# The first MoE in five token blocks instead of six, its temporaries in hand-made rings

## Chip, cores and metric

One core of a Trainium2 chip runs the whole program. The metric is the device time of one execution in microseconds. Engines: PE is the matmul engine (TensorE), PEld its weight loads, DVE the vector engine, ACT the scalar engine, POOL GpSimd, and SP the queue that issues the DMAs.

## What is computed

Attention with a forget bias, then two mixture blocks without routing, on 4 x 576 = 2304 tokens of 512 features:

```python
x = attention(q, k, v, s)                       # 2304 x 512
gate = 1 / (1 + exp(-(x @ w_gate)))             # first MoE, 1536 hidden
x = (gate * (x @ w_val)) @ w_out                # 2304 x 512
h = x @ w_in                                    # second MoE, 2048 hidden
out = (h * cos(h)) @ w_out2                     # 2304 x 512
```

The weights of both MoEs come as 64-bit floats.

## The kernel before

The attention is ordered by a planner at build time (`Plan`, L118) and ends at about 185 us. What follows it, `moe()` (L799), is written out by hand: every engine takes its instructions in the order of two loops, and semaphores make it wait for its operands.

Each value x is kept as two 32-bit parts, a rounded one and the rest (XH and XL, gh and gl, the halves of a weight piece `wp`), and a product is three matmuls, high x high, high x low and low x high (`mm3`, L378). XH and XL hold all tokens, feature by feature: [128, 4, 2304].

The first MoE works on blocks of TB = 384 tokens, NB = 6 of them, and on hidden tiles of 128, 12 of them in six groups (`GROUPS1`, L360: 1, 2, 2, 2, 3 and 2 tiles). `work` (L389) makes the list of items: group by group, in it block by block, in it tile by tile; 72 items. An item's matmuls are `gate_val` (24: gate and value, each 4 feature chunks x 3) and `down1` (12: 4 output chunks x 3). The weights are the stationary side, so a matmul streams the tokens of a block: 384 columns.

The loop at L943 runs one item ahead: `gate_val(i)`, then `down1(i-1)`. Then follow the other engines' instructions: `glu` (ACT: sigmoid sg, L812; DVE: product g, L814; ACT: cast gh, L816), `evac1` of item i-1 (on the last tile of a group its four output chunks are added to `acc`: by ACT copies in the first group, L842, by DVE else, L844 and L846, in the last group with XH by ACT, L848, and XL by POOL, L849, put off to `drain_late`), `glu_lo` (DVE: difference gl, L822), and `background(share)`.

`background` decodes the weights of the next group. A piece (a 128 x 512 tile of a weight) is fetched by a DMA from SP (L308) into one of two `raw` buffers and then takes five operations, among them DVE's L312, L317, L321, L325 and L333, ACT's L313, and POOL's L326 and L334. The number of operations per item, `share`, is set at the first item of a group (L956 to L966): five times the pieces, divided by the items that are left, rounded up.

```python
share = -(-share // (NB * len(GROUPS1[it["gi"]]) - 1))
```

The temporaries come from pools: gh and gl four buffers each (`gp`), sg and g two each and kk one (`tp`), all of 384 columns. Matmul results live in the eight banks of PSUM (one tile, `pw`): four in turn for gate and value, four for the down sums.

The second MoE (L972) has 96 items of the same 384-token blocks: `up2` (12 matmuls of 384 columns), three items later `down2` (9 matmuls of 512 columns, here the tokens are stationary), between them `phase` (ACT: kk, L865), `cosine` (DVE: L870, L871; ACT: L872, L873), `gated` (DVE: L879) and `gated_split` (ACT: gh, L885; POOL: gl, L886). `acc` is used again, in pieces of 512 columns (`evac2`: L907, L909, L914).

Of the kernel before, what the change touches and what calls it, by code (L numbers as in the profile page):

```python
# [244 lines left out]
def kernel(  # L245
# [137 lines left out]
    def xmm(ps, w, b):  # L383
        cols = slice(b * TB, (b + 1) * TB)
        for c in range(NDC):
            fs = slice(c * P, (c + 1) * P)
            mm3(ps[:, 0:TB], w[:, 0, fs], w[:, 1, fs], XH[:, c, cols], XL[:, c, cols], c == 0, c == NDC - 1)

    def work(groups):  # L389
        items = []  # L390
        for gi, gr in enumerate(groups):
            for b in range(NB):
                for fc in gr:
                    items.append(dict(b=b, f=fc, gi=gi, first=fc == gr[0], last=fc == gr[-1], g0=gi == 0, g1=gi == len(groups) - 1))
        return items

    def gate(it):
        it["ps"] = [b[:, 0:TB] for b in pair_a()]
        xmm(it["ps"][0], W["g", it["f"]], it["b"])

    def val(it):
        xmm(it["ps"][1], W["v", it["f"]], it["b"])
# [5 lines left out]
    items1, items2 = work(GROUPS1), work(GROUPS2)  # L408
# [390 lines left out]
    def moe():  # L799
        with ExitStack() as c2:  # L800
            gp = c2.enter_context(tc.tile_pool(name="gp", bufs=4))
            tp = c2.enter_context(tc.tile_pool(name="tp", bufs=2))
# [3 lines left out]
            acc = accp.tile([P, NB, NDC * TB], F32, name="acc")  # L806


            def glu(it):
                pg, pv = it.pop("ps")  # L810
                sg = tp.tile([P, TB], F32, name="sg")
                act.activation(sg, pg, AF.Sigmoid)  # L812
                g = tp.tile([P, TB], F32, name="g")
                dve.tensor_tensor(g, pv, sg, ALU.mult)  # L814
                gh = gp.tile([P, TB], F32R, name="gh")
# [3 lines left out]
            def glu_lo(it):  # L819
                gh, g = it["g"]  # L820
                gl = gp.tile([P, TB], F32R, name="gl")
# [5 lines left out]
            def down1(it, c):  # L827
# [5 lines left out]
                mm3(px[b, c][:, 0:TB], w[:, 0, fs], w[:, 1, fs], gh, gl, it["first"], it["last"])  # L833

            def evac1(it, c):
                b = it["b"]
                if not it["last"]:
                    return
                ps = px.pop((b, c))[:, 0:TB]
                a = acc[:, b, c * TB:(c + 1) * TB]  # L840
# [4 lines left out]
                else:  # L845
                    dve.tensor_tensor(a, ps, a, ALU.add)  # L846
                    xh = XH[:, c, b * TB:(b + 1) * TB]
                    act.copy(xh, a)  # L848
                    late.append(lambda: pool.tensor_tensor(XL[:, c, b * TB:(b + 1) * TB], a, f(xh), ALU.subtract))  # L849
# [6 lines left out]
            def up2(it):  # L856
                b, fc = it["b"], it["f"]
                ph = banks(2, 0, 3)
                xmm(ph, W["i2", fc], b)
                it["ps"] = ph[:, 0:TB]  # L860

            def phase(it):
                h = it["ps"]
                it["kk"] = kk = tp.tile([P, TB], I32, name="kk", bufs=1)
                act.mul(kk, h, 1.0 / (2.0 * math.pi))  # L865

            def cosine(it):
                h, kk = it["ps"], it.pop("kk")
                r = tp.tile([P, TB], F32, name="sg")
# [172 lines left out]
```

## Time and profile before

| | us |
|---|---|
| median of 3 runs | 1045.12 (1044.97 to 1045.98) |
| span of the profiled execution, first to last instruction | 1043.9 |
| PE busy | 1030.7 (99%) |
| PE weight loads busy | 945.7 (91%) |
| DVE busy | 733.4 (70%) |
| ACT busy | 471.9 (45%) |
| POOL busy | 442.0 (42%) |

The profiled execution's own time is known by its span alone; the three timed runs lie 1.1 to 2.1 us over it. Busy times of different engines overlap. PE's matmuls overlap each other as well, so their price is read from the distance between two starts and not from the duration of one. Attention takes the first 185 us, the first MoE the time to about 640, the second the rest.

### The profile page before, as it was taken

Reading aid. Unit: us, or ns where it says so; the run is one execution under the profiler, and the core shown is the slowest. Engines: PE = TensorE matmul, PEld = TensorE weight load, DVE = VectorE, ACT = ScalarE, POOL = GpSimd, SP = SyncE. Lnnn points to the kernel's source line nnn. Section 1 sums busy time; section 2 is a strip of 40 time slices with the busy share of each in tenths; the row PEclk is TensorE's granted clock in tenths of the full one; section 3 lists DMA queues with packets and bytes.
Section 4 is the critical chain, followed back from the end, with each engine's and each line's share of the span. In section 5 each row is a group of like instructions: output and inputs, shape, how many; then the busy total and the mean of one; then the engine's idle time right before and its main releaser. Section 6 shows DMA issues by size and latency. Waiting matters only on the chain.

```text
span 1043.9 us, 16751 instructions
## 1 busy us (share of the span) xinstructions
PE 1030.7 (99%) x6116; PEld 945.7 (91%) x6116; DVE 733.4 (70%) x1382; ACT 471.9 (45%) x1060; POOL 442.0 (42%) x518
## 2 busy tenths in 40 slices
PE   8999999999999999999999999999999999999998
PEld 6776777899999999999999999899999999999997
DVE  7788898576646657744443886987688878886565
ACT  4877877342222222222221334666555455544443
POOL 3567876242302214411110674655355535552222
PEclk9999999999999999999999999999999999999999
DMA  7786783221101112201100111111011101100111
GB/s 173 171 194 163 192 183 98 90 84 41 62 21 61 41 41 78 66 22 39 41 21 21 61 62 41 41 61 42 21 61 41 54 28 41 60 2 8 53 61 61
DMA packets 94802, 70.49 MB, mean 68 GB/s; under 512 B 61888, under 2 KB 82752, under 8 KB 94720
## 3 DMA queue, kind: packets, MB, share of 16 engines
q1 hardware_dynamic: 93456, 69.06, 23.8%
q8 instruction: 48, 0.79, 0.3%
q10 hardware_dynamic: 1264, 0.37, 0.2%
q14 instruction: 34, 0.28, 0.1%
HBM read 64.54 MB, written 4.87 MB: 66 GB/s over the span
## 4 chain that ended last, share of the span: by engine, by line
PE 81%; DVE 9%; issue 3%; ACT 3%; POOL 2%; DMA 2%; SPq 0%; DVEq 0%; ACTq 0%; POOLq 0%
PE pw L380 17%; PE pw L381 17%; PE pw L379 17%; PE pw L896 6%; PE pw L898 6%; PE pw L897 6%; PE pw L726 3%; PE pw L687 3%; PE pw L628 3%; PE pw L633 1%; DVE wm L321 1%; POOL XL L849 1%; DVE wm L325 1%; DVE g L814 1%; DVE gl L822 1%
## 5 line engine op out<-in xcount | busy, mean ns | idle before, releaser
L380 PE MATMUL pw<-XL,wp 128*128 128x384 f32 x960 | 322.7, 336 | 0.0
L381 PE MATMUL pw<-XH,wp 128*128 128x384 f32 x960 | 322.7, 336 | 0.0
L379 PE MATMUL pw<-XH,wp 128*128 128x384 f32 x960 | 322.6, 336 | 0.0
L379 PEld LDWEIGHTS pw<-XH,wp 128*128 128x128 f32 x960 | 180.1, 188 | 3.8 <-DVE g L879 0.2
L380 PEld LDWEIGHTS pw<-XL,wp 128*128 128x128 f32 x960 | 180.0, 188 | 3.6
L326 POOL TENSOR_TENSOR wm<-wm,wx 128x512 int32<-128x512 int32 x68 | 90.6, 1332 | 212.6 <-DVE wm L325 211.3
L381 PEld LDWEIGHTS pw<-XH,wp 128*128 128x128 f32 x960 | 180.1, 188 | 0.0
L886 POOL TENSOR_TENSOR gl<-g,gh 128x384 fp32r<-128x384 f32 x96 | 108.7, 1133 | 150.9 <-ACT gh L885 150.7
L334 POOL TENSOR_TENSOR wp<-wm,wp 128x512 fp32r<-128x512 f32 x68 | 101.4, 1491 | 156.7 <-DVE wp L333 149.5
L814 DVE TENSOR_TENSOR g<-pw,sg 128x384 f32<-128x384 f32 x72 | 40.0, 556 | 145.1 <-PE pw L381 132.6
L898 PE MATMUL pw<-wp,gl 128*128 128x512 f32 x288 | 112.2, 390 | 0.5 <-POOL gl L886 0.5
L896 PE MATMUL pw<-wp,gh 128*128 128x512 f32 x288 | 112.2, 389 | 0.1
L897 PE MATMUL pw<-wp,gh 128*128 128x512 f32 x288 | 112.1, 389 | 0.0
L816 ACT CAST gh<-g 128x384 fp32r<-128x384 f32 x72 | 37.0, 514 | 146.7 <-DVE g L814 146.7
L871 DVE SCALAR_TENSOR_TENSOR sg<-kk,sg 128x384 f32<-128x384 int32 x96 | 100.5, 1047 | 3.3
L872 ACT ACTIVATE sg<-sg 128x384 f32<-128x384 f32 x96 | 50.5, 526 | 107.4 <-DVE sg L871 107.3
L379 PE MATMUL pw<-gh,wp 128*128 128x384 f32 x288 | 96.8, 336 | 1.4 <-ACT gh L816 1.4
L380 PE MATMUL pw<-gl,wp 128*128 128x384 f32 x288 | 97.2, 338 | 0.8 <-DVE gl L822 0.8
L381 PE MATMUL pw<-gh,wp 128*128 128x384 f32 x288 | 96.2, 334 | 0.0
L313 ACT ACTIVATE wx<-wx,ebias 128x512 int32<-128x512 int32 x68 | 49.2, 723 | 96.1 <-DVE wx L312 93.5
L649 ACT ACTIVATE pu<-pu,nm 128x128 f32<-128x128 f32 (+3 forms) x144 | 82.8, 577 | 20.7 <-DVE nm L645 20.5
L879 DVE SCALAR_TENSOR_TENSOR g<-sg,pw 128x384 f32<-128x384 f32 x96 | 52.7, 549 | 44.8 <-ACT sg L873 44.8
(102 smaller groups left out, 1752.3 us busy)
## 6 DMA issues: line engine op xcount, KB each, us to landing
raw<-in_moe_w_out_dram SPq DMA_DIRECT2D x28, 512.0 KB
CB<-cum_d SPq DMA_DIRECT2D x32, 288.0 KB
raw<-in_moe_w_in_dram SPq DMA_DIRECT2D x16, 512.0 KB
raw<-in_moe_w_gate_dram SPq DMA_DIRECT2D x12, 512.0 KB
raw<-in_moe_w_val_dram SPq DMA_DIRECT2D x12, 512.0 KB
VN<-in_v_dram SPq DMA_DIRECT2D x31, 160.0 KB
Kn<-in_k_dram SPq DMA_DIRECT2D x32, 144.0 KB
rb<-rec_d SPq DMA_DIRECT2D x32, 144.0 KB
```

The source lines that it names most:

```text
L326: pool.tensor_tensor(m, m, st["x"], ALU.add)
L334: pool.tensor_tensor(w[:, 1], m, f(w[:, 0]), ALU.subtract)
L379: pe.matmul(ps, wh, xh, start=first, stop=False)
L380: pe.matmul(ps, wh, xl, start=False, stop=False)
L381: pe.matmul(ps, wl, xh, start=False, stop=last)
L649: act.activation(o, o, AF.Exp, bias=NMT[nm.slot][:, col:col + 1], scale=-1.0, accum_out=SUMS[sums.slot][:, col:col + 1])
L871: dve.scalar_tensor_tensor(r, kk, -TWO_PI_LO, r, ALU.mult, ALU.add)
L879: dve.scalar_tensor_tensor(g, r, -0.5, h, ALU.add, ALU.mult)
L886: pool.tensor_tensor(gl, g, f(gh), ALU.subtract)
L896: pe.matmul(ps, gh[:, ts], w[:, 0], start=it["first"], stop=False)
L897: pe.matmul(ps, gh[:, ts], w[:, 1], start=False, stop=False)
L898: pe.matmul(ps, gl[:, ts], w[:, 0], start=False, stop=it["last"])
```

## The change

The first MoE works on blocks of 464, 464, 464, 464 and 448 tokens, five instead of six (`BLOCKS1`, `WB` is 464); the second keeps six of 384. An item carries its block's first token o and its size n. 60 items take the place of 72. The share of `background` is divided over five blocks instead of six. `acc` is laid out by block: NDC x n columns each. The pools `gp` and `tp` become three tiles of fixed size, GH, GL and TM, of the same bytes. `Slots` hands out parts of them in turn: in the first MoE three slots of 464 for gh and for gl (before: four of 384) and two each for sg and g; in the second MoE the numbers and widths of before. (A line of "..." marks what is left out.)

```diff
+    BLOCKS1 = [(464 * b, 464) for b in range(4)] + [(1856, NT - 1856)]
+    WB = max(n for _, n in BLOCKS1)
     TB = 384
     NB = NT // TB
+    BLOCKS2 = [(TB * b, TB) for b in range(NB)]
...
-    def xmm(ps, w, b):
-        cols = slice(b * TB, (b + 1) * TB)
+    def xmm(ps, w, o, n):
+        cols = slice(o, o + n)
...
-    def work(groups):
+    def work(groups, blocks):
         items = []
         for gi, gr in enumerate(groups):
-            for b in range(NB):
+            for b, (o, n) in enumerate(blocks):
...
-            gp = c2.enter_context(tc.tile_pool(name="gp", bufs=4))
-            tp = c2.enter_context(tc.tile_pool(name="tp", bufs=2))
+            mid = c2.enter_context(tc.tile_pool(name="mid", bufs=1))
...
-            acc = accp.tile([P, NB, NDC * TB], F32, name="acc")
+            acc = accp.tile([P, NDC * NT], F32, name="acc")
+            GH = mid.tile([P, 4 * TB], F32R, name="gh")
+            GL = mid.tile([P, 4 * TB], F32R, name="gl")
+            TM = mid.tile([P, 5 * TB], F32, name="tm")
+
+            class Slots:
+                def __init__(self, t, at, width, n):
+                    self.t, self.at, self.width, self.n, self.used = t, at, width, n, 0
+
+                def tile(self, n):
+                    o = self.at + self.used % self.n * self.width
+                    self.used += 1
+                    return self.t[:, o:o + n]
+
+            gh_r, gl_r = Slots(GH, 0, WB, 3), Slots(GL, 0, WB, 3)
+            sg_r, g_r = Slots(TM, 0, WB, 2), Slots(TM, 2 * WB, WB, 2)
+            gh_s, gl_s = Slots(GH, 0, TB, 4), Slots(GL, 0, TB, 4)
+            sg_s, g_s, kk_s = Slots(TM, 0, TB, 2), Slots(TM, 2 * TB, TB, 2), Slots(TM, 4 * TB, TB, 1)
...
-                sg = tp.tile([P, TB], F32, name="sg")
+                sg = sg_r.tile(it["n"])
...
-                gh = gp.tile([P, TB], F32R, name="gh")
+                gh = gh_r.tile(it["n"])
...
-                mm3(px[b, c][:, 0:TB], w[:, 0, fs], w[:, 1, fs], gh, gl, it["first"], it["last"])
+                mm3(px[b, c][:, 0:it["n"]], w[:, 0, fs], w[:, 1, fs], gh, gl, it["first"], it["last"])
...
-                a = acc[:, b, c * TB:(c + 1) * TB]
+                a = acc[:, NDC * o + c * n:NDC * o + (c + 1) * n]
...
-                    xh = XH[:, c, b * TB:(b + 1) * TB]
+                    xh = XH[:, c, o:o + n]
...
-                it["kk"] = kk = tp.tile([P, TB], I32, name="kk", bufs=1)
+                it["kk"] = kk = kk_s.tile(TB).bitcast(I32)
...
-                a = acc[:, b, c * 512:(c + 1) * 512]
+                a = acc[:, (b * SUB + c) * 512:(b * SUB + c + 1) * 512]
...
-                    share = -(-share // (NB * len(GROUPS1[it["gi"]]) - 1))
+                    share = -(-share // (len(BLOCKS1) * len(GROUPS1[it["gi"]]) - 1))
```

## Rows read from the trace of the kernel before

**Rows 1.** The page's head: busy time of PE, and PE's granted clock in 40 slices.
```profile
PE 1030.7 (99%) x6116; PEld 945.7 (91%) x6116; DVE 733.4 (70%) x1382; ACT 471.9 (45%) x1060; POOL 442.0 (42%) x518
...
PEclk9999999999999999999999999999999999999999
```

**Rows 2.** Busy time by stretch (columns in the first row); clock, DMA share, GB/s.
```profile
core 0: us, PE busy (x) PEld busy (x) DVE busy (x) ACT busy (x) POOL busy (x), PEclk, DMA share, GB/s
197.37:222.36 24.99, 24.99 (x146) 24.99 (x145) 20.18 (x31) 12.74 (x29) 13.07 (x9) 1.00 0.28 87
...
297.32:372.28 74.96, 74.96 (x434) 74.96 (x433) 42.32 (x78) 16.27 (x30) 16.66 (x12) 1.00 0.14 43
372.28:448.40 76.12, 75.77 (x433) 74.88 (x433) 52.14 (x93) 17.46 (x33) 26.18 (x18) 1.00 0.20 63
...
560.84:635.80 74.96, 74.96 (x433) 74.96 (x433) 57.84 (x85) 26.05 (x51) 42.17 (x33) 1.00 0.16 50
653.94:1036.00 382.06, 381.38 (x1922) 348.30 (x1921) 299.13 (x449) 206.37 (x413) 177.13 (x146) 1.00 0.13 41
```

**Rows 3.** PE in order of time, three matmul widths: start, duration of each.
```profile
99.76 0.29 PE L633 MATMUL pw<-KH,QH 128*128 128x288 f32 x1
99.89 0.29 PE L633 MATMUL pw<-KH,QL 128*128 128x288 f32 x1
...
800.80 0.34 PE L379 MATMUL pw<-XH,wp 128*128 128x384 f32 x1
...
802.92 0.39 PE L896 MATMUL pw<-wp,gh 128*128 128x512 f32 x1
...
804.96 0.34 PE L379 MATMUL pw<-XH,wp 128*128 128x384 f32 x1
```

**Rows 4.** Start of the first MoE, in order of time, ACT and PE.
```profile
191.79 1.28 ACT L812 ACT_TABLE_LOAD   x1 [5.61 <-DVE XL L768]
...
193.61 0.34 PE L381 MATMUL pw<-XH,wp 128*128 128x384 f32 x1
...
195.63 0.34 PE L381 MATMUL pw<-gh,wp 128*128 128x384 f32 x1
```

**Rows 5.** Fourth group, in order of time, DVE and ACT.
```profile
430.50 0.56 DVE L814 TENSOR_TENSOR g<-pw,sg 128x384 f32<-128x384 f32 x1 [1.50 <-ACT sg L812]
...
436.78 0.72 ACT L313 ACTIVATE wx<-wx,ebias 128x512 int32<-128x512 int32 x1 [5.18 <-DVE wx L312]
...
439.05 0.56 DVE L822 TENSOR_TENSOR gl<-g,gh 128x384 fp32r<-128x384 f32 x1 [0.58 <-ACT gh L816]
...
444.39 0.55 DVE L814 TENSOR_TENSOR g<-pw,sg 128x384 f32<-128x384 f32 x1
```

**Rows 6.** Groups by shape, whole span: count | busy us, mean ns | idle before.
```profile
L886 POOL TENSOR_TENSOR gl<-g,gh 128x384 fp32r<-128x384 f32 x96 | 108.7, 1133 | 150.9 <-ACT gh L885 150.7
...
L844 DVE TENSOR_TENSOR acc<-pw,acc 128x384 f32<-128x384 f32 x96 | 49.7, 550 | 0.0
...
L822 DVE TENSOR_TENSOR gl<-g,gh 128x384 fp32r<-128x384 f32 x72 | 41.1, 571 | 24.9 <-ACT gh L816 24.9
...
L909 DVE TENSOR_TENSOR acc<-pw,acc 128x512 f32<-128x512 f32 x36 | 22.5, 677 | 0.0
...
L907 ACT COPY acc<-pw 128x512 f32<-128x512 f32 x18 | 9.9, 590 | 0.3
L842 ACT COPY acc<-pw 128x384 f32<-128x384 f32 x24 | 9.9, 486 | 0.0
```

**Rows 7.** End of the first MoE, in order of time, POOL, DVE and PE.
```profile
631.32 5.32 POOL L849 TENSOR_TENSOR XL<-acc,XH 128x384 fp32r<-128x384 f32 x4 [1.84 <-ACT XH L848]
...
639.17 0.43 DVE L333 CAST wp<-wm 128x512 fp32r<-128x512 f32 x1 [3.42 <-POOL wm L326]
...
639.79 0.34 PE L381 MATMUL pw<-XH,wp 128*128 128x384 f32 x1
...
643.43 0.33 PE L379 MATMUL pw<-XH,wp 128*128 128x384 f32 x1
```

**Rows 8.** Groups by shape, 185 to 640 us, DVE: the costliest decode step.
```profile
L325 DVE SCALAR_TENSOR_TENSOR wm<-raw,wm 128x512 int32<-128x512 int32 x41 | 47.1, 1150 | 1.1
```

More of the change, by code (lines that the diff above doesn't have):

```diff
@@ L381, in mm3 @@
         pe.matmul(ps, wl, xh, start=False, stop=last)
-    def xmm(ps, w, b):
-        cols = slice(b * TB, (b + 1) * TB)
+    def xmm(ps, w, o, n):
+        cols = slice(o, o + n)
         for c in range(NDC):
             fs = slice(c * P, (c + 1) * P)
-            mm3(ps[:, 0:TB], w[:, 0, fs], w[:, 1, fs], XH[:, c, cols], XL[:, c, cols], c == 0, c == NDC - 1)
-    def work(groups):
+            mm3(ps[:, 0:n], w[:, 0, fs], w[:, 1, fs], XH[:, c, cols], XL[:, c, cols], c == 0, c == NDC - 1)
+    def work(groups, blocks):
         items = []
         for gi, gr in enumerate(groups):
-            for b in range(NB):
+            for b, (o, n) in enumerate(blocks):
                 for fc in gr:
-                    items.append(dict(b=b, f=fc, gi=gi, first=fc == gr[0], last=fc == gr[-1], g0=gi == 0, g1=gi == len(groups) - 1))
+                    items.append(dict(b=b, o=o, n=n, f=fc, gi=gi, first=fc == gr[0], last=fc == gr[-1], g0=gi == 0, g1=gi == len(groups) - 1))
         return items
     def gate(it):
-        it["ps"] = [b[:, 0:TB] for b in pair_a()]
-        xmm(it["ps"][0], W["g", it["f"]], it["b"])
+        it["ps"] = [b[:, 0:it["n"]] for b in pair_a()]
+        xmm(it["ps"][0], W["g", it["f"]], it["o"], it["n"])
     def val(it):
-        xmm(it["ps"][1], W["v", it["f"]], it["b"])
+        xmm(it["ps"][1], W["v", it["f"]], it["o"], it["n"])
     def gate_val(it):
@@ L406, in gate_val @@
         val(it)
-    items1, items2 = work(GROUPS1), work(GROUPS2)
+    items1, items2 = work(GROUPS1, BLOCKS1), work(GROUPS2, BLOCKS2)
     def attention():
@@ L805, in moe @@
             rings.append(c2.enter_context(tc.tile_pool(name="ring", bufs=13)))
-            acc = accp.tile([P, NB, NDC * TB], F32, name="acc")
+            acc = accp.tile([P, NDC * NT], F32, name="acc")
[13 more added lines that the diff above has]
+            sg_s, g_s, kk_s = Slots(TM, 0, TB, 2), Slots(TM, 2 * TB, TB, 2), Slots(TM, 4 * TB, TB, 1)
             def glu(it):
                 pg, pv = it.pop("ps")
-                sg = tp.tile([P, TB], F32, name="sg")
+                sg = sg_r.tile(it["n"])
                 act.activation(sg, pg, AF.Sigmoid)
-                g = tp.tile([P, TB], F32, name="g")
+                g = g_r.tile(it["n"])
                 dve.tensor_tensor(g, pv, sg, ALU.mult)
-                gh = gp.tile([P, TB], F32R, name="gh")
+                gh = gh_r.tile(it["n"])
                 act.copy(gh, g)
@@ L820, in glu_lo @@
                 gh, g = it["g"]
-                gl = gp.tile([P, TB], F32R, name="gl")
+                gl = gl_r.tile(it["n"])
                 dve.tensor_tensor(gl, g, f(gh), ALU.subtract)
@@ L868, in cosine @@
                 h, kk = it["ps"], it.pop("kk")
-                r = tp.tile([P, TB], F32, name="sg")
+                r = sg_s.tile(TB)
                 dve.scalar_tensor_tensor(r, kk, -TWO_PI_HI, h, ALU.mult, ALU.add)
@@ L877, in gated @@
                 h, r = it.pop("ps"), it.pop("sq")
-                it["g"] = g = tp.tile([P, TB], F32, name="g")
+                it["g"] = g = g_s.tile(TB)
                 dve.scalar_tensor_tensor(g, r, -0.5, h, ALU.add, ALU.mult)
@@ L882, in gated_split @@
                 g = it["g"]
-                gh = gp.tile([P, TB], F32R, name="gh")
-                gl = gp.tile([P, TB], F32R, name="gl")
+                gh, gl = gh_s.tile(TB), gl_s.tile(TB)
                 act.copy(gh, g)
```

8 lines of the change are left out of this document (4 added, 4 removed).

## The prediction

> **What bounds the kernel now.** I read the page's first two parts, then busy time by stage, then the matmul spacing, then the places where TensorE (PE) stood. Over the span PE is busy 99% of the time and its granted clock is at its upper level, 2.4 GHz, in all 40 slices [rows 1, 2]. So nothing is to be won from a colder clock, and a change pays only by giving PE fewer or cheaper matmuls or by closing the few gaps.
>
> By stage [rows 2]: the first MoE takes its six weight groups between 185 and 640 us. One item (one block of tokens, one hidden tile) is 36 matmuls. In the third group 12 items, 432 matmuls, take 74.96 us, in the sixth the same: 173.5 ns a matmul, with PE busy in every microsecond of it. Only the fourth group is longer, 76.12 us for the same 12 items. VectorE (DVE) is busy 56 to 81% in these and the first group. PE sets the pace and the others hide behind it.
>
> **The matmul's price.** What matters is how the spacing depends on the columns [rows 3]. Nine matmuls of 512 columns take 2.04 us from the first start to the start after them, 226.7 ns each. Those of 384 columns in the first MoE take 173.5 (above). The slope is (226.7-173.5)/128 = 0.415 ns a column, which is 2.4 GHz, and what is left is a fixed 14.1 ns a matmul. The third width, 288 columns, checks it: 0.13 us apart by rows of two decimals, where the line gives 133.7 ns. On this line 464 columns cost 206.7 ns and 448 cost 200.1.
>
> **The change part by part.**
> *Fewer, wider matmuls.* Each of the 12 hidden tiles needs 36 matmuls a block, so 12 x 36 = 432 weight passes over all tokens. A pass is now 6 x 173.5 = 1041.1 ns and becomes 4 x 206.7 + 200.1 = 1026.9, or 14.1 less: 432 x 14.1 = **-6.1 us**, all of it on the path. The columns streamed are the same; 432 fixed parts go. Bounds: if none of the 14.1 ns is fixed, the gain is 0. The 384-column matmuls of the second MoE, which alternate with 512-column ones, stand 2.12 us/12 = 176.7 ns apart [rows 3]; a line through those has a fixed part of 26.7 ns and a gain of 11.5 us, and if instead the new widths took on these 3.2 ns each, 60 x 36 of them would cost 6.9 us and the gain would be gone. I take 14.1, since the row it comes from is this stage's own.
>
> The row shows a fixed part of 14.1 ns. The Trainium skill, "TensorE: Matmul & The Clock Gate", section "Part 2: What happens when you issue a matmul", gives a warm gap of N/2.4 plus about 2.5 ns, which speaks against this change: an estimate by that figure is 432 x 2.5 = 1.1 us instead of 6.1. The trace disagrees with it at 384 and 512 columns.
>
> *The start.* ACT loads its table at 191.79, its first sigmoid waits for that, and by then PE has run through the two items that it may do ahead: from the last matmul of the second at 193.61 to the fourth one behind it at 195.63 is 2.02 us instead of 3 x 0.17, 1.5 us of standing [rows 4]. Two items of 24 matmuls ahead now last 48 x 206.7 ns = 9.9 us instead of 8.3, 1.6 more, while the chain behind the table load (sigmoid, product, cast, difference) grows by about 0.3. I leave 0.3 us of stall: **-1.2**.
>
> *The fourth group.* It is 1.16 us over its neighbours [rows 2]. Its DVE queue is full: from one product g (L814) to that two items later is 13.89 us [rows 5], against 2 x 6.25 of PE, and the sigmoid on ACT stands behind a decode step (L313) that itself waits for DVE. These two items hold 2 products, 2 differences, 4 accumulations and 10 decode operations, five each. DVE's accumulation is 550 ns for 384 columns and 677 for 512 [rows 6], so 79 more for 464; eight such operations add 0.63 us, ACT's shares in the chain about 0.26 (four operations, by 486 and 590 ns [rows 6]). The decode share stays five. So 14.8 us, against 2 x 36 x 206.7 ns = 14.9 of PE: it just keeps up, **-1.1**.
>
> *The background in the other groups.* The share of decode operations per item rises with fewer items: 6 to 8 in the first group, 3 to 4 in the second and third, 2 to 3 in the fifth, 4 to 5 in the last; with each go its DMA issues on SP and POOL's two steps a weight piece, the same number in all. Per microsecond that is nearly the same, since an item grows from 6.25 to 7.44 us. The first group is the crowded one: DVE is busy 20.18 of 24.99 us [rows 2]. Of its 31 instructions in these four items 8 are products and differences at 0.57 [rows 6], so 23 decode operations took 15.6 us, 0.68 each. Eight of them, the wider product and difference and the 0.58 that DVE stands between these two [rows 5] are 7.3 us, inside 7.44. What waits behind DVE is the next product, then the cast, then the down matmuls. These come 36 matmuls, 7.4 us, after the product can start and need about 2 us of chain, so 5.5 us of lateness is hidden.
>
> *The end of the stage.* The 12 down matmuls of the last item should start at 639.96 and end before 642.05, but the next begins at 643.43: 1.4 us [rows 7]. DVE stood 3.42 us for POOL, which had four XL differences in a row (5.32 us), then the decode steps; the last product came after that. XL gets wider, but PE's work ahead too, and one more decode operation is queued: I leave the 1.4. For this and the first and last group together I add **+0.7**, half of what this place shows, between 0 and 2.8.
>
> *Rings and layout.* Where they were four buffers, gh and gl have three slots. A slot is written again three items later, when the down matmuls that read it are done (they run one item behind), so this costs nothing; PE is the cover. The rest (sg, g, kk and the second MoE's slots) keeps its depth, and the second MoE its blocks. The first kk now lies over the last product g and so waits for its difference gl, some 0.6 us; what comes of this kk feeds PE three items later, 12 us, so that is covered. The fourth batch's XH and XL are needed 96 matmuls into the stage (19.8 us) instead of 132 (22.9); the last of them ends just ahead of 191.79, where ACT's wait for it ends [rows 4], 6 us into the stage: covered.
>
> The sum: -6.1 - 1.2 - 1.1 + 0.7 = -7.7 on the profiled span of 1043.9, so 1036.2. The runs' median, 1045.12, is 1.2 over that span; I take the 1.2 as lying around it and get **1037.4**.
>
> **The rivals.**
> 1. *Crowded decode in the first group.* Its 30 decode operations fall into four items, whose 7.44 us less 1.87 for product, difference and the wait between them leave 22.3 us. At x us each DVE overruns by 30x - 22.3, and beyond the 5.5 that are hidden PE stands: from x = 0.93. For it: the step L325 takes 1.15 on average in this stage [rows 8], and the fourth group's two items give 0.83 with all waits (13.89, less 5.6 for the two items' own eight operations and two waits, over ten). Against: 0.68 above. Midway, at 1.04, PE stands 3.4 us: 1040.8, still faster. Chance 0.13.
> 2. *No fixed part, or the slower spacing.* With no gain a matmul the other terms leave -1.6: 1043.5; with the second MoE's 3.2 ns more, 1044.4. Three widths on one line speak against it. Chance 0.10, within 0.2%. The Trainium skill, "TensorE: Matmul & The Clock Gate", in the section named above, stands between: by its figure the time would be 1042.4.
> 3. *Slower: the width is rounded up.* All matmul widths in the trace are multiples of 32 columns (three of them in [rows 3]), and 464 = 14.5 x 32 is not. Should PE stream it as 480, it costs 213.4 ns, a pass is 4 x 213.4 + 200.1 = 1053.7, and 432 x 12.6 ns = +5.4; with the other terms +3.8: 1048.9. It decides from 211 ns on. No row speaks for it but that none excludes it. Chance 0.08.
> 4. *Slower: one tile, one order.* GH, GL and TM are now one tile each. If a write waits for all readers of the tile and not of the slot, each cosine of the second MoE would wait for POOL's gl (1.13 us [rows 6]), where DVE has 0.90 us free an item (382.06 - 299.13 us over the 92 items of that stretch, 12 x 176.7 + 9 x 226.7 ns = 4.16 us each [rows 2]): 96 x 0.23 = +22 us, 1060. Against it: XL, one tile too, is written by POOL from 631.32 on [rows 7], in the last microseconds of the sixth group, while PE reads other columns of it without a break [rows 2]. Chance 0.04.
>
> **How the numbers follow.** The forecast has 0.65. About 0.2%, 2.1 us, is what a measurement of this kernel can tell from no change. Forecast and rival 1 lie below 1043.0: faster 0.78; rival 2: same 0.10; rivals 3 and 4: slower 0.12. The range: downwards the end's 1.4 and my 0.7 may vanish, 1035.3, rounded to 1035.0; upwards it takes in rival 1 with 1.2 over its middle, 1042.0. Rivals 2 to 4 are left out, 0.22.
>
> **What would show it.** Right: 464-column matmuls 206.7 ns apart, items of 7.44 us, the first MoE about 7 us shorter, the fourth group's ten items without a gap, a stall under 0.5 us at the start, the second MoE unchanged. Wrong: a spacing of 210 or more (rivals 2, 3), PE waiting for gh or gl in the first group (rival 1), DVE waiting for POOL before L870 (rival 4).

## The result, and the profile after

| | before | after |
|---|---|---|
| median, us | 1045.05 (4 runs, 1044.66 to 1045.98) | 1051.31 (4 runs, 1050.29 to 1052.00) |
| ratio to before, 95% interval | | 1.0060 (1.0045 to 1.0074) |
| span of the profiled execution, us | 1043.9 | 1049.2 |

The five blocks are slower by 0.6%. The first line of the page after, where [rows 1] stood before:

```profile
PE 1033.4 (98%) x5684; PEld 903.2 (86%) x5684; DVE 736.2 (70%) x1338; ACT 466.9 (44%) x1028; POOL 445.3 (42%) x514
```

PE runs 432 matmuls less and is busy 2.7 us more. So the matmuls did not get cheaper in sum, and PE stands longer besides.

Busy time by stretch, PE alone, the kernel after: the six groups of the first MoE, its last twelve down matmuls, the second MoE (start:end, length, PE busy (matmuls), granted clock, DMA share, GB/s):

```profile
186.19:229.08 42.89, 42.89 (x209) 1.00 0.31 98
229.08:304.31 75.23, 75.23 (x362) 1.00 0.15 47
304.31:379.64 75.33, 75.33 (x361) 1.00 0.14 43
379.64:454.88 75.24, 75.24 (x361) 1.00 0.20 64
454.88:567.72 112.84, 112.84 (x541) 1.00 0.09 29
567.72:645.66 77.94, 74.40 (x350) 0.98 0.18 54
645.66:648.70 3.04, 2.81 (x13) 1.00 0.00 0
648.70:1049.20 400.50, 395.55 (x1993) 1.00 0.13 41
```

The same cuts in the kernel before give 74.96, 74.96, 76.13 and 112.44 us for the second to the fifth group and 2.77 for the last down matmuls. Its first group, sixth group and second MoE:

```profile
185.36:228.60 43.24, 42.27 (x244) 1.00 0.32 101
...
567.09:640.66 73.57, 73.03 (x421) 1.00 0.18 58
...
643.43:1043.90 400.47, 395.93 (x1993) 1.00 0.13 41
```

Two things are to be read off. First, in the groups where PE never stands (the second, third and fifth) the stretch is 0.3 to 0.4 us *longer* than before: 75.33 us for 72 passes over the tokens is 1046.3 ns a pass, where it was 1041.1 and the prediction had 1026.9. Second, the sixth group is 4.4 us longer, PE is idle for 3.5 us of it and the clock is below 1. Since the cuts fall between items, its stretch even streams 2688 columns fewer than before, which is 1.1 us at 2.4 GHz, and the first group's 1920 more, 0.8 us. The first and the fourth group are shorter, as forecast, and the second MoE is as it was. The sum over the first MoE rises from 458.07 to 462.51 us; attention took 0.8 us more.

**The spacing.** The gate and value matmuls of one item in each of the five blocks, third group (24 matmuls a row):

```profile
304.31:309.42 5.11, 5.11 (x25) 1.00 0.01 3
319.46:324.48 5.02, 5.02 (x25) 1.00 0.00 0
334.56:339.60 5.04, 5.04 (x25) 1.00 0.24 71
349.81:354.93 5.12, 5.12 (x26) 1.00 0.00 0
364.81:369.67 4.86, 4.86 (x26) 1.00 0.34 106
```

Divided by 24 that is 213, 209, 210 and 213 ns for the four blocks of 464 columns and 202 for the one of 448, instead of 206.7 and 200.1. (Counts of 25 and 26 take in matmuls that reach over an edge.) Three of the blocks of 464 keep their value in every hidden tile; the fourth has 211 ns in nine of the twelve tiles and 213 in three (both tiles of this group and that of the first); why is open. The compiled program puts XH at byte 16512 of each partition and XL at 53376, both 128 bytes into a stretch of 256. A block of 464 columns is 1856 bytes, 7 x 256 + 64, so the blocks start 128, 192, 0 and 64 bytes into 256. Blocks of 384 columns are 1536 bytes, 6 x 256: they all start at 128. The down matmuls read gh and gl, whose slots of 464 start at 192, 0 and 64, and go with the slot in the same way (209 to 213 ns).

**The sixth group.** PE in order of time, after:

```profile
625.95 0.37 PE L384 MATMUL pw<-XH,wp 128*128 128x448 f32 x1
628.17 0.47 PE L382 MATMUL pw<-gh,wp 128*128 128x464 f32 x1 [1.85 <-ACT gh L835]
...
629.40 0.59 PE L384 MATMUL pw<-gh,wp 128*128 128x464 f32 x1
629.79 0.59 PE L382 MATMUL pw<-gh,wp 128*128 128x464 f32 x1
```

PE waits 1.85 us for gh, then for gl, and after that some matmuls are 0.39 us apart instead of 0.21: from 629.40 to 632.10 the mean granted clock is 0.52, that is, the lower of the two levels (1.2 GHz). Seven such matmuls cost 1.2 us on top of the wait. The other engines just before that, same kernel:

```profile
617.75 5.83 POOL L868 TENSOR_TENSOR XL<-acc,XH 128x464 fp32r<-128x464 f32 x4 [2.04 <-ACT XH L867]
...
619.50 1.42 DVE L336 CAST wp<-wm 128x512 fp32r<-128x512 f32 x1
620.84 1.69 DVE L324 SCALAR_TENSOR_TENSOR wm<-raw,wm 128x512 int32<-128x512 int32 x1
...
623.55 1.73 POOL L337 TENSOR_TENSOR wp<-wm,wp 128x512 fp32r<-128x512 f32 x1
...
624.05 1.51 DVE L315 TENSOR_SCALAR wx<-raw 128x512 int32<-128x512 int32 x1
...
625.66 0.72 ACT L316 ACTIVATE wx<-wx,ebias 128x512 int32<-128x512 int32 x1 [5.80 <-DVE wx L315]
626.29 0.54 ACT L831 ACTIVATE tm<-pw 128x464 f32<-128x464 f32 x1
626.86 0.64 DVE L833 TENSOR_TENSOR tm<-pw,tm 128x464 f32<-128x464 f32 x1 [1.29 <-ACT tm L831]
```

Read from the bottom: the product (L833) waits for the sigmoid (L831), that stands behind ACT's half of the exponent step (L316), which waits for DVE's half (L315), and this is DVE's last decode operation of the item. It is late because most of DVE's operations beside POOL's XL differences, and beside the split step (L337) that POOL does next, take 1.4 to 1.7 us; in the run with the late XL, below, the same take 0.43 (L336), 0.69 (L324) and 0.41 (L315). The Trainium skill, "SBUF — State Buffer", section "SBUF: two separate sides", says that DVE and POOL share a pair of ports that one instruction of either holds to its end, and of DVE's names those in a two-port mode or with two inputs in SBUF. The rows fit it: L336, L324 and L315 are 1.0 to 1.1 us longer than in that run, while one XL difference takes 5.83/4 = 1.46. In which mode L336 and L315 run, no row shows.

### The profile page after: what moved, and what is told of

Its sections match the earlier page's. It is cut to its first block, busy times and chain, and to the rows that moved or that the text cites. A ratio compares the mean times of both kernels' runs of the same rounds, so it can differ in the third digit from the quotient of the medians.

```text
span 1049.2 us, 15775 instructions
## 1 busy us (share of the span) xinstructions
PE 1033.4 (98%) x5684; PEld 903.2 (86%) x5684; DVE 736.2 (70%) x1338; ACT 466.9 (44%) x1028; POOL 445.3 (42%) x514
## 4 chain that ended last, share of the span: by engine, by line
PE 86%; DVE 5%; DMA 2%; POOL 2%; issue 2%; ACT 2%; SPq 0%; DVEq 0%; POOLq 0%; ACTq 0%
PE pw L383 19%; PE pw L384 19%; PE pw L382 19%; PE pw L916 6%; PE pw L914 6%; PE pw L915 6%; PE pw L729 3%; PE pw L690 3%; PE pw L631 2%; PE pw L636 1%; DMA rb<-rec_d 1%; DVE wx L315 1%; DVE acc L865 1%; DMA raw<-in_moe_w_out_dram 1%; DVE wp L336 1%
## 5 line engine op out<-in xcount | busy, mean ns | idle before, releaser
L383 PE MATMUL pw<-XL,wp 128*128 128x464 f32 (+2 forms) x864 | 308.0, 356 | 0.0
L382 PE MATMUL pw<-XH,wp 128*128 128x464 f32 (+2 forms) x864 | 307.8, 356 | 0.0
L384 PE MATMUL pw<-XH,wp 128*128 128x464 f32 (+2 forms) x864 | 307.8, 356 | 0.0
L382 PEld LDWEIGHTS pw<-XH,wp 128*128 128x128 f32 x864 | 162.0, 187 | 14.2
L904 POOL TENSOR_TENSOR gl<-tm,gh 128x384 fp32r<-128x384 f32 x96 | 108.9, 1134 | 150.8 <-ACT gh L903 150.7
L384 PEld LDWEIGHTS pw<-XH,wp 128*128 128x128 f32 x864 | 162.0, 187 | 10.3
L337 POOL TENSOR_TENSOR wp<-wm,wp 128x512 fp32r<-128x512 f32 x68 | 103.9, 1527 | 149.9 <-DVE wp L336 148.1
L833 DVE TENSOR_TENSOR tm<-pw,tm 128x464 f32<-128x464 f32 (+1 forms) x60 | 38.3, 638 | 149.9 <-PE pw L384 134.9
L316 ACT ACTIVATE wx<-wx,ebias 128x512 int32<-128x512 int32 x68 | 49.2, 724 | 123.8 <-DVE wx L315 122.8
L890 DVE SCALAR_TENSOR_TENSOR tm<-tm 128x384 f32<-128x384 int32 x96 | 100.5, 1046 | 3.3
L891 ACT ACTIVATE tm<-tm 128x384 f32<-128x384 f32 x96 | 50.5, 526 | 107.7 <-DVE tm L890 107.6
L382 PE MATMUL pw<-gh,wp 128*128 128x464 f32 (+1 forms) x240 | 89.7, 374 | 3.1 <-ACT gh L835 3.1
L383 PE MATMUL pw<-gl,wp 128*128 128x464 f32 (+1 forms) x240 | 90.0, 375 | 0.6 <-DVE gl L841 0.6
L384 PE MATMUL pw<-gh,wp 128*128 128x464 f32 (+1 forms) x240 | 89.6, 373 | 0.0
L898 DVE SCALAR_TENSOR_TENSOR tm<-tm,pw 128x384 f32<-128x384 f32 x96 | 52.8, 550 | 43.6 <-ACT tm L892 43.6
```

Source lines behind the costliest of these rows:

```text
L337: pool.tensor_tensor(w[:, 1], m, f(w[:, 0]), ALU.subtract)
L382: pe.matmul(ps, wh, xh, start=first, stop=False)
L383: pe.matmul(ps, wh, xl, start=False, stop=False)
L384: pe.matmul(ps, wl, xh, start=False, stop=last)
L890: dve.scalar_tensor_tensor(r, kk, -TWO_PI_LO, r, ALU.mult, ALU.add)
L898: dve.scalar_tensor_tensor(g, r, -0.5, h, ALU.add, ALU.mult)
```

## The experiments

Two questions: why are the wider matmuls dearer than the line, and why does PE stand in the last group? For the first, the theory is that the place of the operands within 256 bytes sets an extra time; its rivals are a width rounded up, one dearer value at all places, and the new rings. For the second, the theory is the order of work in that group (XL ahead of the decode steps, and which step comes last); its rivals are that wider items hold too much work for DVE anyway, or that the rings do it.

**Six blocks with the new rings.**

```diff
-    BLOCKS1 = [(464 * b, 464) for b in range(4)] + [(1856, NT - 1856)]
+    BLOCKS1 = [(384 * b, 384) for b in range(6)]
```

> The changed kernel with its rings, layout of acc and slots, but with six blocks of 384 again. Theory A (the loss lies in the block width alone: spacing of the matmuls and the longer last group): 1045.1 us, the time of the kernel before within 0.15%, matmuls of 384 columns 173.5 ns apart, four places of stall as before. Rival B (the hand-made rings, with three slots instead of four for gh and gl, cost waits of their own): 1046.5 or more, with PE or ACT waiting before gh or gl outside the four places of before.

1043.70 us in 10 runs, ratio 0.9988 (0.9975 to 1.0002), the first MoE 458.06 us long, 173 and 174 ns a matmul. Rings, layout and three slots instead of four cost nothing that these runs can tell, as the prediction had it.

**Blocks of 480 columns.** 480 is a multiple of 32, and the starts are 128 and 0 bytes into 256 in turn.

```diff
+    BLOCKS1 = [(480 * b, 480) for b in range(4)] + [(1920, NT - 1920)]
```

> Five blocks of 480, 480, 480, 480 and 384 tokens; nothing else changed. In the changed kernel matmuls of 464 columns stand 210.7 ns apart on average, not 206.7. Theory A1 (a width that is no multiple of 32 columns is rounded up): 480 columns 213.4 ns apart and 384 columns 173.5, so a pass over all tokens is 1027 ns and the first MoE's matmuls take 7.8 us less than with 464; time near 1044. Theory A2 (the spacing depends on where in SBUF a block's first column lies, in steps of 64 columns or 256 bytes): 480 columns spread over two values by block, some of them above 214, and less is gained, 1045 to 1050. Rival A3 (anything wider than 384 simply costs 4 ns more): 480 columns 217.5 ns apart in every block, time near 1051. Stalls in the last group remain in all three.

1050.93 us, ratio 1.0058 (1.0041 to 1.0075). The blocks show 215.9, 218.2, 215.8 and 217.8 to 218.3 ns: two values in turn, both above the 213.4 of the line. So rounding up to 32 columns is not it: 480 columns need none, and they too lie above the line and depend on the start. Two values in turn are theory A2's, but the time is as long as rival A3 had it.

**The XL differences behind the decode steps.**

```diff
-                drain_late()
                 nxt = it["gi"] + 1
...
                 else:
                     background(share)
+                drain_late()
```

> The changed kernel; only the four XL differences on POOL are issued after the decode operations of the item and not ahead of them. Theory C (PE's stalls in the last group come from DVE's decode operations that stand behind POOL's four wide XL differences): the stalls of about 0.5, 2.2 and 1.9 us near 611, 626 and 645 us, and the half clock after the second, go or shrink to under 1 us together; 1046 to 1048 us. Rival D (the fifth decode operation alone fills DVE, whatever POOL does): the stalls stay within 1 us of their sum, 1051. The matmul spacing stays as it is in both.

1047.25 us in 10 runs, ratio 1.0023 (1.0013 to 1.0032), 4 us less than the change alone. Of the same place in the group, in order of time:

```profile
618.06 0.43 DVE L336 CAST wp<-wm 128x512 fp32r<-128x512 f32 x1
618.39 0.69 DVE L324 SCALAR_TENSOR_TENSOR wm<-raw,wm 128x512 int32<-128x512 int32 x1
...
620.70 0.41 DVE L315 TENSOR_SCALAR wx<-raw 128x512 int32<-128x512 int32 x1
...
621.21 0.72 ACT L316 ACTIVATE wx<-wx,ebias 128x512 int32<-128x512 int32 x1 [2.78 <-DVE wx L315]
...
622.23 5.21 POOL L868 TENSOR_TENSOR XL<-acc,XH 128x464 fp32r<-128x464 f32 x4
```

Three of the four decode operations between product and exponent step have their short durations back (L328, with 1.66 us, has not), and ACT's half of the exponent step begins 4.6 us after the start of the last pair of accumulations, where it was 7.6. PE's waits for gh and gl in this MoE fall from 3.7 to 1.7 us. XL now comes later, and at the start of the second MoE PE waits 1.8 us for POOL's gl, where it was 1.1.

**Five blocks of 464 that all start at 192.** They start at tokens 16, 464, 912, 1360 and 1808 (so they overlap by 16, and the first 16 and the last 32 tokens are left out).

```diff
+    BLOCKS1 = [(16 + 448 * b, 464) for b in range(5)]
```

> Five blocks of 464 columns that start at tokens 16, 464, 912, 1360 and 1808, so that every block starts at the same place within 64 columns (256 bytes), that of the second block of the changed kernel. Tokens 0 to 15 and 2272 to 2303 are left out of the first MoE, and the seams are computed twice and mixed. Theory A2 (the start sets the spacing): gate and value matmuls of all five blocks 209.0 ns apart, where the changed kernel has 213.2, 209.0, 210.0 and 211.2 by block. Rivals A1 and A3 (the width alone, or the place in the order): the blocks keep different values, or all have 211 and more. Time not compared, since there are 16 columns more in the fifth block.

Gate and value in two of the five blocks, third group:

```profile
306.12:311.13 5.01, 5.01 (x25) 1.00 0.02 3
...
351.31:356.32 5.01, 5.01 (x26) 1.00 0.00 0
```

208.9 ns in all five, the value that only the block at 192 had in the change. The start is what makes the difference between blocks. The other 2.2 ns over the line stay.

**Five widths at one start.** The starts are all at 128.

```diff
+    BLOCKS1 = [(0, 496), (512, 432), (960, 416), (1408, 400), (1856, NT - 1856)]
```

> Blocks of 496, 432, 416, 400 and 448 tokens, all starting at a multiple of 64 tokens, so at the same place within 256 bytes as the five-block kernel's first block; 112 tokens between the blocks are left out of the first MoE (they keep the attention's values), and the product g is written over sg, so the time is not one to compare. Read is the spacing of the gate and value matmuls by block. Theory L (a fixed part and 2.4 GHz, the line of the prediction): 220.8, 194.1, 187.4, 180.8 and 200.8 ns. Theory W (widths that are not whole multiples of 128 columns pay more, by how they lie in 256 bytes): 448 again 202.2, and the others 2 to 6 ns above the line: 496 at 223 to 227, 432 at 196 to 200, 416 at 189 to 193, 400 at 183 to 187.

```profile
301.17:306.45 5.28, 5.28 (x26) 1.00 0.01 3
316.43:321.07 4.64, 4.64 (x26) 1.00 0.00 0
330.25:334.73 4.48, 4.48 (x25) 1.00 0.15 40
343.65:348.06 4.41, 4.41 (x26) 1.00 0.00 0
357.26:362.12 4.86, 4.86 (x25) 1.00 0.34 107
```

496, 432 and 416 columns lie on the line (220.0, 193.3, 186.7 ns), 400 and 448 lie 2 to 3 ns above it (183.8, 202.5 by these rows). Not every hidden tile is the same: 496 columns take 226.7 ns in three of twelve, 400 columns 180.0 in two. Theory L holds for three of the five widths and theory W for the other two. What makes a width cheap at a given start stays open.

**384 columns at five starts.**

```diff
+    BLOCKS1 = [(400 * b, 384) for b in range(5)] + [(2000, NT - 2000)]
```

> Blocks of 384 tokens at 0, 400, 800, 1200, 1600 and one of 304 at 2000, so that the 384-column matmuls start 0, 64, 128, 192 and again 0 bytes further within 256 bytes; 80 tokens between them are left out of the first MoE (they keep the attention's values), so the time is not one to compare. Read is the spacing of gate and value matmuls by block. Theory S (the start alone sets the extra time, at any width): 173.2 in the first and fifth block and up to 4 ns other values in the second to fourth. Theory W (a width of whole 128 columns pays nothing wherever it starts, the start counts only for widths with a remainder): 173.2 in all five.

173.3 ns at 192, 173.1 at 0, 176.0 at 64, and 173.2 to 176.7 at 128, by the hidden tile. So 384 columns are not free of it either, but the effect is 3.6 ns at most, and the kernel before has 173.2 throughout its first MoE. Since the blocks at 128 take up to 176.7 here and not there, the start alone does not set the time; what else does is open.

**Four blocks of 512 and one of 256**, with the late XL. The product goes over sg so that three slots of 512 fit.

```diff
+    BLOCKS1 = [(0, 256)] + [(256 + 512 * b, 512) for b in range(4)]
...
-            sg_r, g_r = Slots(TM, 0, WB, 2), Slots(TM, 2 * WB, WB, 2)
+            sg_r = Slots(TM, 0, WB, 3)
...
-                g = g_r.tile(it["n"])
+                g = sg
```

> Blocks of 256, 512, 512, 512 and 512 tokens, XL queued behind the decode steps as in the run with the late XL, the product g written over sg so that rings of 512 fit. Theory W or L: 512 columns cost 226.7 ns, 256 cost 120.7, a pass over the tokens 1027.5 ns instead of 1041.1: 432 x 13.6 ns = 5.9 us less than the kernel before, and 1 us from the start and 1 from the fourth group, so 1037 to 1040 us, faster. Theory Q (wider items, whatever their matmuls cost, leave longer waits at the ends of groups because one item holds more of DVE's and POOL's work): PE stands 5 us or more in the first MoE, 1043 us or more.

1044.50 us in 10 runs, ratio 0.9990 (0.9981 to 1.0000): neither. PE waits 0.7 us in the first MoE, not 5, but gate and value, whose XH blocks all start at 128, take 233.3 ns, 6.6 over the line:

```profile
330.41:336.01 5.60, 5.60 (x26) 1.00 0.32 90
```

The down matmuls of the same width, whose gh slots all start at 192, take 226.7 to 228.3. Both theories had left the start out.

**Six blocks with the late XL.**

> Six blocks of 384 with the rings, and XL queued behind the decode steps. Theory C (the four XL on POOL ahead of the decode steps make PE wait at the end of the first MoE): the six blocks lose their 1.4 us there and 0.5 to 1.5 us are gained over the 1043.7 of the six blocks with rings: 1042 to 1043. Rival: the order helps only where items are wider: 1043.5 to 1044, no change.

1043.38 us, ratio 0.9979 (0.9966 to 0.9991), the first MoE 456.68 us, 1.4 less than with the rings alone. The time lies between the two expectations, and its interval overlaps that of the rings alone; the 0.2% are no gain of wider blocks.

**Four blocks of 496 and one of 320.** Late XL, product over sg, slots 512 wide. The blocks of 496 start at 128, 64, 0 and 192.

> Blocks of 320, 496, 496, 496 and 496 tokens, XL queued behind the decode steps, the product over sg, slots 512 wide. In the run with five widths 496 columns cost 220.2 ns, on the line of the prediction, where 464 cost 6.5 ns more than it. Theory W (the width decides and 496 is a cheap one): gate and value 220 to 222 in the four wide blocks, a pass over the tokens about 1028 to 1035 ns, 36 x 12 of them 445 us instead of 450: 1037 to 1040 us, faster by 0.5%. Theory S (the start within 256 bytes adds its own here, since the blocks start 128, 64, 0 and 192 bytes into it): one or more of the four at 224 to 227 ns, 1041 to 1045 us.

1042.65 us, ratio 0.9972 (0.9962 to 0.9982). One item of each:

```profile
315.00:320.44 5.44, 5.44 (x27) 1.00 0.00 0
323.11:328.47 5.36, 5.36 (x25) 1.00 0.32 101
...
355.45:360.74 5.29, 5.29 (x26) 1.00 0.01 3
```

Only the block at 192 is at 220 ns; the others show 223 to 227 (the one at 128 changes between 220 and 226.5 with the hidden tile). Theory S again.

**XL by DVE instead of POOL**, late, at 464 columns, and the same with the blocks of 496.

```diff
-                    late.append(lambda: pool.tensor_tensor(XL[:, c, o:o + n], a, f(xh), ALU.subtract))
+                    late.append(lambda: dve.tensor_tensor(XL[:, c, o:o + n], a, f(xh), ALU.subtract))
```

> The five blocks of 464 and 448 with XL queued behind the decode steps, and computed by DVE instead of POOL. Theory P (POOL's XL doubles the time of the DVE instructions beside it, so DVE loses as much as it would take to do XL itself): PE's waits in the last group stay under 2 us as with XL on POOL, 1046 to 1048 us; the DVE decode steps that took 1.4 to 1.7 us beside XL take 0.4 to 0.8. Rival (DVE is simply full in the last group, XL there is 3 us more of it): PE waits 3 us or more, 1049 to 1051 us.

> Both edits: blocks of 320 and four of 496, XL by DVE behind the decode steps. Theory W with P: as the blocks of 496 alone, within 1 us. Theory S with P: the same. Rival (DVE full): 2 us or more above the blocks of 496 with XL on POOL.

1048.11 us, ratio 1.0027 (1.0018 to 1.0036), and 1044.84, ratio 0.9992 (0.9980 to 1.0004). Beside XL the decode operations no longer stretch, which theory P had said, but the last product stands behind four XL (3.38 us on DVE) and at 464 columns PE waits 3.0 us there, which the rival had said. It is 0.9 us worse than XL on POOL at 464 columns, where the intervals overlap, and 2.2 at 496: no gain.

**The blocks of 512 with XH and XL 64 bytes higher**, so that they start at 192, too.

```diff
+    base.tile([P, 16], F32R, name="shift")
     XH = base.tile([P, NDC, NT], F32R, name="XH")
...
+            mid.tile([P, 48], F32R, name="shift2")
             GH = mid.tile([P, 4 * TB], F32R, name="gh")
```

> As the blocks of 256 and four of 512 (gate and value there 233.4 ns apart, down matmuls 226.7 to 228.3), but XH and XL lie 64 bytes higher by an unused tile of 16 columns ahead of them, so that every block starts 192 bytes into 256 instead of 128; gh and gl keep their 192. Theory S (the moving operand's start within 256 bytes sets the extra time, 192 is the cheap one): gate and value fall to 226.7 to 228.3 in the four wide blocks, 24 x 12 x 4 x 5 to 6.7 ns = 5.8 to 7.7 us less than without the shift: 1036.5 to 1039 us, faster than the kernel before by 0.6 to 0.8%. Rival (the extra belongs to XH and XL or to these matmuls' weights, not to the start): 233 again, 1044 to 1045 us.

The control has the same edit with six blocks of 384:

> Six blocks of 384 with the same shift and the late XL. Theory S and W: 384 columns cost 173.2 at the starts 128, 192 and 0 and 176.0 at 64 in the run with five starts, so nothing changes in the first MoE: 1042.5 to 1044 us, as without the shift. Rival (the shift helps by something else, the weights' places or the second MoE's matmuls): 1 us or more below that.

1040.27 us, ratio 0.9953 (0.9939 to 0.9966); the control with six blocks 1044.43, ratio 0.9996 (0.9987 to 1.0005). Both times lie above what theory S had expected. Gate and value of 512 columns fall to 226.7 to 227.8 in eight of twelve hidden tiles. The other four show 231 to 233. In this kernel the first three of the sixteen weight buffers had moved to 0 within 256, so the weights' place was the next suspect.

**The weights' place.** The unused bytes stand right after XL instead, so that all weight buffers are at 192 again.

```diff
     XL = base.tile([P, NDC, NT], F32R, name="XL")
+    base.tile([P, 48], F32R, name="shift2")
```

> As the shifted blocks of 256 and 512, but the unused bytes stand so that the three weight pieces of the first ring, too, start 192 bytes into 256 as they do in the kernel before (in the shifted run they started at 0, and four of the twelve hidden tiles showed 231 to 233 ns instead of 226.7). Theory S for both operands: all hidden tiles at 226.7 to 228.3, 1.5 to 2.5 us less in the first MoE, and the second MoE's 2 us are back: 1036 to 1038.5 us. Rival (those four tiles are slow for another reason): 231 to 233 in them again, 1040 us.

> Six blocks of 384 with XH, XL, gh, gl and all weight pieces 192 bytes into 256, XL late: the control for the widths. Theory S: 173.2 in all hidden tiles as before (they showed 175 to 176.7 in three of twelve with the shifted weight ring), 1042.5 to 1044 us. Rival (the places alone bring what the blocks of 512 show): 1040 us or less.

All twelve hidden tiles are at 226.7 to 227.8, on the line, and the first MoE is 449.21 us long (before: 458.07). But the time is 1040.59, ratio 0.9955 (0.9943 to 0.9968), since the second MoE grew to 403.46 us (before: 400.47); control 1045.45, ratio 0.9997 (0.9988 to 1.0006), also above what was expected. The first part of the expectation held, the second did not.

**Only XH and XL moved**, by two small tiles taken from behind them to ahead of them; all else at the addresses of the kernel before.

```diff
+    for e in (896, 895):
+        ebias[e] = base.tile([P, 1], F32, name=f"ebias{e}")
     XH = base.tile([P, NDC, NT], F32R, name="XH")
```

> As the run with all operands 192 bytes into 256, but made by moving the two 32-byte bias tiles ahead of XH and XL, so that XH and XL lie 64 bytes higher and everything else at the very addresses of the kernel before. There the first MoE was 9 us shorter and the second 3 us longer, its 512-column matmuls with the weights moving at 232 to 234 ns instead of 227. Theory G (what makes the second MoE longer is the 256 bytes by which gh, gl and the weights lie higher): its matmuls are at 227 again, its time at 395 to 397 us as in the kernel before, 1036 to 1038 us in all. Theory X (it is XH's and XL's own start, which the second MoE's first matmuls share): 232 to 234 again, 399 us, 1040 us.

> The control: six blocks of 384 with late XL and the same two bias tiles moved. The first MoE as without the move (456 to 457 us). Theory G: the second MoE 395 to 397, 1042.5 to 1044 us. Theory X: the second MoE 397.5 or more, 1044.5 to 1046 us.

1039.74 us, ratio 0.9948 (0.9935 to 0.9960), the fastest here; control 1045.34, ratio 1.0003 (0.9994 to 1.0012). First and second MoE and one item of 512 columns, blocks of 512:

```profile
184.92:634.35 449.43, 448.73 (x2189) 1.00 0.16 52
634.35:1037.80 403.45, 397.98 (x1993) 1.00 0.12 41
...
327.70:333.14 5.44, 5.44 (x25) 1.00 0.28 87
```

and the first and second MoE of its control with six blocks:

```profile
185.19:641.32 456.13, 454.96 (x2620) 1.00 0.17 51
641.32:1042.90 401.58, 397.70 (x1993) 1.00 0.13 41
```

By these cuts the kernel before has 400.47 us in the second MoE, not the expectation's 395 to 397, so only differences can be compared. They are theory X's: the start of XH and XL costs the second MoE 2.4 us of PE's busy time (395.2 us with six blocks and the late XL unmoved, 397.7 in the control). It lies in the 512-column down matmuls, though none of their own operands moved: nine of them take 2.08 us instead of 2.04 [rows 3], while twelve of the 384-column ones before them take 2.106 instead of 2.120. The blocks of 512 lose 1.6 us more in the second MoE, a wait of PE for a gl that POOL makes behind XL; the control has no such wait. Between these two kernels, the same but for block width (and the product over sg), the first MoE differs by 6.7 us.

**One decode operation fewer in the last group's second item.** A piece's five operations go exponent, mantissa, split, mantissa, sign. With a share of five each item holds one whole piece, so the same step stands last in every item of the group: in the change it is the exponent step. This run shifts that by one and leaves all else of the change as it is.

```diff
-                    background(share)
+                    background(share - (it["g1"] and it["b"] == 0))
```

> The changed kernel with one decode operation fewer in the last group's second item, so that from there on an item's five operations end with the sign step and begin with the exponent step, instead of ending with it; the order of XL stays. The exponent step has an ACT part that stands ahead of the next item's sigmoid. Theory H (with a share of five, one whole piece an item, the exponent step comes last in every item and its ACT part holds the sigmoid up until DVE is through with all five): in the items after a block's accumulation the sigmoid comes 4 us or more earlier, the product directly behind DVE's last decode step, PE's stand shrinks by about 1.3 us in each of the last group's two or three places: 1047 to 1049.5 us. Rival (DVE's own lateness beside XL on POOL is all, the sigmoid would have been early enough): 1050.5 to 1052 us, PE's waits in the last group as before.

1042.25 us in 7 runs, ratio 0.9974 (0.9962 to 0.9986): 9 us less than the change, where theory H had said 2 to 4. The sixth group, the last down matmuls and the second MoE:

```profile
567.91:639.83 71.92, 71.92 (x349) 1.00 0.19 59
639.83:642.28 2.45, 2.45 (x14) 1.00 0.01 3
642.28:1041.40 399.12, 395.27 (x1993) 1.00 0.13 42
```

The sixth group is 6.0 us shorter than in the change and PE does not stand in it at all; the end is shorter by 0.6, the second MoE by 1.4. A loaded item shows how:

```profile
614.50 0.42 DVE L315 TENSOR_SCALAR wx<-raw 128x512 int32<-128x512 int32 x1
614.84 1.42 DVE L320 TENSOR_SCALAR wm<-raw 128x512 int32<-128x512 int32 x1
615.11 0.72 ACT L316 ACTIVATE wx<-wx,ebias 128x512 int32<-128x512 int32 x1
...
619.23 1.67 DVE L328 SCALAR_TENSOR_TENSOR wm<-raw,wm 128x512 int32<-128x512 int32 x1
620.83 0.63 DVE L833 TENSOR_TENSOR tm<-pw,tm 128x464 f32<-128x464 f32 x1
```

Beside XL most of DVE's operations are as long as in the change (1.4 to 1.7 us), but the exponent step is first, ACT has done its half at 615.8, and the product follows DVE's last decode step without a wait. In the change DVE stood 1.29 us there, for ACT's half and the sigmoid, and 1.29 and 1.32 us at the same place of the two items before, the second time with no XL running. From one product to that two items later DVE took 17.6 us in the change (609.30 to 626.86), against 15.1 us of PE for two items (a fifth of a group's 75.3); here it takes 15.15 (605.68 to 620.83). So DVE keeps up, and nothing of the wait, of the half-speed matmuls after it or of the lateness handed to the next items is left. That is why the gain is more than the 1.3 us a place that theory H had counted. The blocks of 512 with XH moved and this order together were not tried.

## Why the prediction was wrong

*What bounds the kernel* held: PE sets the pace and a stretch without a gap is matmuls times spacing. In the changed kernel's last group alone DVE set it, with 17.6 us for two items against PE's 15.1.

*Fewer, wider matmuls, -6.1 us*, failed, and failed most. The line through 384 and 512 columns was taken to hold between them; its third point (288) could not show a deviation, being read from rows of two decimals. Its two points stood at different starts, besides: 384 columns of XH at 128, but 512 columns of a weight piece, in the second MoE, at 192. At 128, 512 columns take 233.3 ns. Measured: 1046.3 ns a pass instead of 1026.9. Times 432 passes that is +2.2 us (432 x 5.2 ns) instead of -6.1, 8.3 us off. The prediction knew that widths could be dearer, but only by rounding up to 32 columns (rival 3); the blocks of 480 speak against this, though the price from which it decides, 211 ns, was about reached (208.9 to 213.3). Rival 2's "slower spacing", 3.2 ns a matmul, comes nearest in size: (1046.3 - 1026.9)/5 is 3.9. What the prediction did not ask is where each block starts: with 384 columns every block starts at the same place within 256 bytes, with 464 each at another. That wider blocks can gain is shown by those of 512 with all operands at 192: 226.7 ns, and 6.7 us less than the control in the first MoE. At 464 columns no start tried here gave the 206.7: at 192 it stayed 2.2 ns above, and why is open. By the formula that the Trainium skill, "TensorE: Matmul & The Clock Gate", section "Part 2: What happens when you issue a matmul", gives for the gap of an isolated matmul, 464 columns would take an estimated 195.8 ns; the runs show 13 to 18 ns more.

*The start, -1.2*, held: the sigmoid is in time, no stand is left (first group PE busy throughout, 42.89 of 42.89 us, where the cut before had 42.27 of 43.24). The kernel before had lost 1.6 us there: its 240 matmuls, at 173.2 and 174.3 ns, make 41.65 of the 43.24.

*The fourth group, -1.1*, held: its gap is gone (75.24 of 75.24 us), and the accumulation took 637 ns where 629 was estimated.

*The background in the other groups* held in the first five groups: rival 1 did not come, PE waits for nothing in the first group.

*The end of the stage, +0.7* for the last group, was mis-sized. Against the run with the shifted order the last group, the end and the second MoE hold 8.0 us more, of standing and of half-speed matmuls; the kernel before stood about 1.4 us at the end [rows 7] and was 1.3 us longer in the second MoE (400.47 against 399.12 us). That leaves about 5.3 us for the change, 4.6 over the term. The step counted the share as "one more decode operation" and not as what it does to the order: from four to five it no longer moves round through a piece's steps but stands still, with the exponent step, and its ACT half ahead of the sigmoid, always last. Two causes meet there, XL beside the decode steps and the exponent step at their end; taking away the first won back 4 us (late XL), taking away the second 9 (the shift), with XL beside the decode steps as before. With the second alone PE still waited 1.7 us in the first MoE; with the first alone it did not wait in the last group.

*Rings and layout* held (six blocks with rings), and with it the *against* of rival 4: the second MoE takes 400.50 us for 400.47.

The sum: 1037.4 + 8.3 + 4.6 = 1050.3; the runs of the change lie 2.1 us over the profiled span where 1.2 was taken, which makes 1051.2 of 1051.31. That it meets the measured time so closely is partly luck: the 0.8 us more of attention is not in it, and the start won 1.6 us instead of 1.2, which offsets half of that.

## What to carry to other kernels

Before the tile width of a matmul stream is changed, work out where each new tile starts in memory, for the moving operand and for the weights, and price the width from rows at those starts; a line through two widths, each read at one start, says nothing of other starts. When a fixed list of background steps is dealt out in equal shares, look which step each share ends with: a share equal to the list's period freezes one step in front of the next item's work. Here one operation moved was worth 9 us, and the best width at the best start 6.7 in the first MoE.

## What was not expected of the hardware

- A matmul's spacing depends on its operands' start within 256 bytes: 512 columns took 233.3 ns at 128 and 226.7 at 192, 464 columns 208.9 (192), 210 (0), 211 to 213 (64) and 213 (128). With the weights at 192, the start 192 was the cheapest of those tried for 464, 496 and 512 columns. The weights' start counts as well (512 columns took 231 to 233 ns where weight buffers lay at 0).
- At one start the spacing is no straight line over the width: at 128, 416, 432 and, in most hidden tiles, 496 columns lie on the prediction's line, 400, 448, 464, 480 and 512 lie 2 to 7 ns above, 256 lies 2 to 3 below (117.8). Why is open.
- What is cheap for one stream can be dear for a mix: XH and XL at 192 left 384 columns of the first MoE at 173.3 ns, but in the second, where they alternate with 512-column matmuls, the move cost 2.4 us.
- A wait of 1.85 us was followed by matmuls at the lower granted clock, 0.39 us apart instead of 0.21; the wait cost 1.2 us more than it lasted.
